# Attention backward for grouped queries: pieces of dV and dK with two heads and four rows c instead of four heads and two

## The chip, the cores and the metric

The kernel runs on one core of one Trainium2 chip. The metric is the time of one execution on the device, in microseconds; the median of several executions is compared.

## The reference

For each of 32 batches there are 32 query heads of 4 rows, 4 key and value heads of 2048 rows, and a head dimension of 128, all bf16. Eight query heads share one key head. The kernel returns the attention's output and the gradients of q, k and v.

```python
B, Hq, Hkv, Sq, Sk, D = 32, 32, 4, 4, 2048, 128
def _fwd_reference(q, k, v):
    k = jnp.repeat(k, rep, axis=1)
    v = jnp.repeat(v, rep, axis=1)
    scores = jnp.einsum("bhqd,bhkd->bhqk", q, k) * D ** -0.5
    p = _softmax(scores, axis=-1)
    return jnp.einsum("bhqk,bhkd->bhqd", p, v)
def reference(q, k, v, grad_out):
    _out, _vjp = jax.vjp(_f, q, k, v)
    _grads = _vjp(grad_out)
    return (_out0, *[jnp.asarray(_g) for _g in _grads])
```

## The kernel before

**Layout.** A batch's 32 heads by 4 rows of q fill the 128 partitions: 32 partitions (G) for each key head h. Key row number p*16 + c of a head is partition p, place c (C = 16). So k and v of a batch are tiles of 128 partitions by 4 heads by 16 c by 128, 2 MB each, loaded by SP in four transfers (LK, LV; L154 and L160).

**Steps.** A batch b goes through named steps, each a small function; a table maps the names to the functions. QDT turns q and grad_out (PE transposes, copied by DVE). KT0 to KT7 and VT0 to VT7 turn k and v in pieces of eight 128x128 blocks (L181, copied by DVE at L183). Sa and Sb are the scores, two halves of 1024 columns (c 0 to 7 and 8 to 15), with a maximum on DVE; EXa and EXb are the exponentials on ACT, into `e0` and `e1`. ETa and ETb turn `e` (L248); O multiplies it with v (L264), writes the output, and forms `delta`. dPa and dPb multiply grad_out with turned v, and DVE makes `ds0` and `ds1` from it (L338). dSTa, dSTb turn `ds` (L248); dQ multiplies it with k. NRM makes the reciprocals and, on POOL, the tiles `dop` and `qp` (L231): grad_out and q scaled by row, each key head's 32 partitions in one of two columns blocks, so that heads 0 and 1 lie in partitions 0 to 63 and heads 2 and 3 in partitions 64 to 127, the rest zero.

**The pieces that are changed.** dV0 to dV7 and dK0 to dK7 call `outer`. dV is `e` transposed times `dop`, dK is `ds` transposed times `qp`. Each piece takes two PSUM banks, runs four matmuls (L303) with 64 partitions of contraction and 256 columns, copies the 128x1024 result on ACT into an output tile (L307), and gives the banks back. In the kernel before, a piece i holds all four heads for c = 2i and 2i + 1: for each c one matmul on partitions 0 to 63 (heads 0, 1; `a = 0`) and one on partitions 64 to 127 (heads 2, 3; `a = 1`), each `a` into its own bank. One output tile holds a batch's dV or dK (16 KB a partition); there are four such tiles (`outp`). When the eighth piece is copied, two stores of 1 MB go out on POOL's queue, one for each pair of heads (L326). In the last batch each half of c is stored when its four pieces are copied (L319).

**Order.** All steps stand in an order written out by hand: HEAD for the first three batches, STEADY once for each batch, TAIL for the last five. Within STEADY, steps of the next batch (`+`), the batch before (`-`) and the one after next (`+2`) are interleaved; each engine runs its part in that order. POOL's queue carries NRM's multiplications, the stores of all outputs, and every fourth batch's loads of q and grad_out.

`Banks` deals out the eight PSUM banks in that order when the program is built; the tile framework puts in the waits between engines.

Of the kernel before, what the change touches and what calls it, by code (L numbers as in the profile page):

```python
# [9 lines left out]
BF16 = mybir.dt.bfloat16  # L10
# [5 lines left out]

HEAD = """
LK@0 LV@0 QDT@0 KT4@0 KT6@0 KT2@0 KT0@0 KT3@0 KT5@0 KT1@0 KT7@0 LK@1 LV@1 VT2@0 Sa@0 Sb@0 VT5@0 VT3@0 EXb@0 VT4@0 EXa@0 VT0@0 QDT@1 KT4@1
KT6@1 KT2@1 KT0@1 NRM@0 ETb@0 ETa@0 VT7@0 KT3@1 VT6@0 VT1@0 dV7@0 O@0 dV5@0 dPb@0 dV1@0 KT5@1 KT1@1 dV3@0 dV6@0 dPa@0 KT7@1 dV2@0 LK@2 LV@2
VT2@1 dV4@0 Sa@1 dV0@0 Sb@1 dK7@0 VT5@1 VT3@1 EXb@1 dSTa@0 VT4@1 EXa@1 VT0@1 QDT@2 dSTb@0 KT4@2 dK1@0 dK6@0 KT6@2 KT2@2 KT0@2 NRM@1 dK0@0 dQ@0  # L20
dK3@0 dK5@0 dK2@0 ETb@1 ETa@1 VT7@1 KT3@2 VT6@1 VT1@1 dV7@1 dK4@0 O@1 dV5@1 dPb@1 dV1@1 KT5@2 KT1@2 dV3@1 dV6@1 dPa@1 KT7@2 dV2@1 LK@3 LV@3
VT2@2 dV4@1 Sa@2 dV0@1 Sb@2 dK7@1 VT5@2 VT3@2 EXb@2 dSTa@1 VT4@2 EXa@2 VT0@2 QDT@3 dSTb@1 KT4@3 dK1@1 dK6@1 KT6@3 KT2@3 KT0@3 NRM@2 dK0@1 dQ@1
dK3@1 dK5@1 dK2@1 ETb@2 ETa@2 VT7@2 KT3@3 VT6@2 VT1@2 dV7@2 dK4@1 O@2 dV5@2 dPb@2 dV1@2 KT5@3 KT1@3 dV3@2 dV6@2 dPa@2 KT7@3 dV2@2 LK@4 LV@4
VT2@3 dV4@2 Sa@3 dV0@2 Sb@3 dK7@2 VT5@3 VT3@3 EXb@3
"""
HEAD_ITERATIONS = 3

STEADY = """
dSTa- VT4 EXa VT0 QDT+ dSTb- KT4+ dK1- dK6- KT6+ KT2+ KT0+ NRM dK0- dQ- dK3- dK5- dK2- ETb ETa VT7 KT3+ VT6 VT1
dV7 dK4- O dV5 dPb dV1 KT5+ KT1+ dV3 dV6 dPa KT7+ dV2 LK+2 LV+2 VT2+ dV4 Sa+ dV0 Sb+ dK7 VT5+ VT3+ EXb+  # L30
"""

TAIL = """
dSTa@-6 VT4@-5 EXa@-5 VT0@-5 QDT@-4 dSTb@-6 KT4@-4 dK1@-6 dK6@-6 KT6@-4 KT2@-4 KT0@-4 NRM@-5 dK0@-6 dQ@-6 dK3@-6 dK5@-6 dK2@-6 ETb@-5 ETa@-5 VT7@-5 KT3@-4 VT6@-5 VT1@-5
dV7@-5 dK4@-6 O@-5 dV5@-5 dPb@-5 dV1@-5 KT5@-4 KT1@-4 dV3@-5 dV6@-5 dPa@-5 KT7@-4 dV2@-5 LK@-3 LV@-3 VT2@-4 dV4@-5 Sa@-4 dV0@-5 Sb@-4 dK7@-5 VT5@-4 VT3@-4 EXb@-4
dSTa@-5 VT4@-4 EXa@-4 VT0@-4 QDT@-3 dSTb@-5 KT4@-3 dK1@-5 dK6@-5 KT6@-3 KT2@-3 KT0@-3 NRM@-4 dK0@-5 dQ@-5 dK3@-5 dK5@-5 dK2@-5 ETb@-4 ETa@-4 VT7@-4 KT3@-3 VT6@-4 VT1@-4
dV7@-4 dK4@-5 O@-4 dV5@-4 dPb@-4 dV1@-4 KT5@-3 KT1@-3 dV3@-4 dV6@-4 dPa@-4 KT7@-3 dV2@-4 LK@-2 LV@-2 VT2@-3 dV4@-4 Sa@-3 dV0@-4 Sb@-3 dK7@-4 VT5@-3 VT3@-3 EXb@-3
dSTa@-4 VT4@-3 EXa@-3 VT0@-3 QDT@-2 dSTb@-4 KT4@-2 dK1@-4 dK6@-4 KT6@-2 KT2@-2 KT0@-2 NRM@-3 dK0@-4 dQ@-4 dK3@-4 dK5@-4 dK2@-4 ETb@-3 ETa@-3 VT7@-3 KT3@-2 VT6@-3 VT1@-3  # L40
dV7@-3 dK4@-4 O@-3 dV5@-3 dPb@-3 dV1@-3 KT5@-2 KT1@-2 dV3@-3 dV6@-3 dPa@-3 KT7@-2 dV2@-3 LK@-1 LV@-1 VT2@-2 dV4@-3 Sa@-2 dV0@-3 Sb@-2 dK7@-3 VT5@-2 VT3@-2 EXb@-2
dSTa@-3 VT4@-2 EXa@-2 VT0@-2 QDT@-1 dSTb@-3 KT4@-1 dK1@-3 dK6@-3 KT6@-1 KT2@-1 KT0@-1 NRM@-2 dK0@-3 dQ@-3 dK3@-3 dK5@-3 dK2@-3 ETb@-2 ETa@-2 VT7@-2 KT3@-1 VT6@-2 VT1@-2
dV7@-2 dK4@-3 O@-2 dV5@-2 dPb@-2 dV1@-2 KT5@-1 KT1@-1 dV3@-2 dV6@-2 dPa@-2 KT7@-1 dV2@-2 VT2@-1 dV4@-2 Sa@-1 dV0@-2 Sb@-1 dK7@-2 VT5@-1 VT3@-1 EXb@-1 dSTa@-2 VT4@-1
EXa@-1 VT0@-1 dSTb@-2 dK1@-2 dK6@-2 NRM@-1 dK0@-2 dQ@-2 dK3@-2 dK5@-2 dK2@-2 ETb@-1 ETa@-1 VT7@-1 VT6@-1 VT1@-1 dV7@-1 dK4@-2 O@-1 dV5@-1 dPb@-1 dV1@-1 dV3@-1 dV6@-1
dPa@-1 dV2@-1 dV4@-1 dV0@-1 dK7@-1 dSTa@-1 dSTb@-1 dK1@-1 dK6@-1 dK0@-1 dQ@-1 dK3@-1 dK5@-1 dK2@-1 dK4@-1
"""
TAIL_ITERATIONS = 5

# [33 lines left out]
def kernel(ctx: ExitStack, tc: tile.TileContext, q, k, v, grad_out, out_0, out_1, out_2, out_3):  # L82
    nc = tc.nc
    B, Hq, Sq, D = q.shape
    NH, Sk = k.shape[1], k.shape[2]
    P = 128
    G = Hq * Sq // NH
    C = Sk // P
# [12 lines left out]
    et_pool = ctx.enter_context(tc.tile_pool(name="etp", bufs=2))  # L101
    ds_pool = ctx.enter_context(tc.tile_pool(name="dsp", bufs=2))
    dst_pool = ctx.enter_context(tc.tile_pool(name="dstp", bufs=2))
    out_pool = ctx.enter_context(tc.tile_pool(name="outp", bufs=4))
    io_pool = ctx.enter_context(tc.tile_pool(name="iop", bufs=3))
    qd_pool = ctx.enter_context(tc.tile_pool(name="qdp", bufs=2))
    sm_pool = ctx.enter_context(tc.tile_pool(name="smp", bufs=3))
# [2 lines left out]
    banks = Banks(ps_pool.tile([P, 8, 512], FP32, name="banks"))  # L110
# [21 lines left out]
    store = nc.gpsimd  # L132
# [158 lines left out]

    def outer(S, x, y, dst, name, i, b, copy):

        if name not in S:
            S[name + "left"] = 8
            S[name] = out_pool.tile([P, NH, C, D], BF16, name=name, tag="outp")
        t = banks.take(2)
        ps = banks.ap(t).rearrange("p a (j c d) -> p a j c d", j=2, c=2)
        for c in range(2):
            u = P * ((2 * i + c) % 8)  # L300
            for a in range(2):
                r = slice(2 * G * a, 2 * G * a + 2 * G)
                nc.tensor.matmul(  # L303
                    ps[:, a, :, c, :], lhsT=S[f"{x}{i // 4}"][r, u:u + P], rhs=S[y][r, :, :],
                    start=True, stop=True, tile_position=(2 * G * a, 0),
                )
        copy(  # L307
            out=S[name][:, :, 2 * i:2 * i + 2, :].rearrange("p h c d -> p h (c d)"),
            in_=banks.ap(t).rearrange("p a (j w) -> p (a j) w", j=2),
        )  # L310
        banks.give(t)
        S[name + "left"] -= 1
        if b == B - 1:

            half = f"{name}half{i // 4}"
            S[half] = S.get(half, 4) - 1
            if S[half] == 0:
                c = slice(8 * (i // 4), 8 * (i // 4) + 8)
                store.dma_start(  # L319
                    out=dst[b].rearrange("p h (c d) -> p h c d", d=D)[:, :, c, :].rearrange("p h c d -> p h (c d)"),  # L320
                    in_=S[name][:, :, c, :].rearrange("p h c d -> p h (c d)"),
                )
        elif S[name + "left"] == 0:
            o = S.pop(name)
            for a in range(2):
                store.dma_start(out=dst[b][:, 2 * a:2 * a + 2, :], in_=o[:, 2 * a:2 * a + 2].rearrange("p h c d -> p h (c d)"))  # L326

    def dV(b, i, copy=nc.scalar.copy):
        outer(st[b], "e", "dop", dv_v, "dv", i, b, copy)

    def dK(b, i, copy=nc.scalar.copy):
        outer(st[b], "ds", "qp", dk_v, "dk", i, b, copy)
# [21 lines left out]
    for w in STEADY.split():  # L354
        ahead = 0
        for mark, n in (("+3", 3), ("+2", 2), ("+", 1), ("-2", -2), ("-", -1)):
            if w.endswith(mark):
                w, ahead = w[:-len(mark)], n
# [3 lines left out]
    with tc.manual_schedule():  # L362

        for w in HEAD.split():
            w, b = w.split("@")
# [5 lines left out]
        for w in TAIL.split():  # L371
            w, b = w.split("@")
# [31 lines left out]
```

## Time and profile before

| | |
|---|---|
| median of 3 runs | 700.63 us (699.89 to 701.72) |
| the profiled execution's own time | 698.71 us |
| its span, first to last instruction | 696.7 us |
| granted TensorE clock | 0.98 |
| PE matmul busy | 626.0 us (90%) |
| DVE, ACT, POOL busy | 584.5, 569.1, 302.7 us |
| L303 matmuls, dV and dK | 1024 and 1024, busy 99.3 and 86.4 us |
| L307 ACT copies, dV and dK | 256 and 256, mean 1028 and 1025 ns |
| moved by DMA | 274.44 MB, mean 394 GB/s |

The profile is one execution. Busy time of an engine is the union of its instructions' times; matmuls overlap in a pipeline, so a group's busy time is less than its count times its mean. "Granted clock" is the share of TensorE's full clock that the throttle let through. An idle time is named after what ended it, so "PE banks L181 <- ACT dv L307" is PE at line 181 waiting for an ACT copy of line 307. The sum of an engine's busy time says little by itself: what counts is which wait ends last in a stretch.

### The profile page before, as it was taken

Reading aid. Unit: us, or ns where it says so; the run is one execution under the profiler, and the core shown is the slowest. Engines: PE = TensorE matmul, PEld = TensorE weight load, DVE = VectorE, ACT = ScalarE, POOL = GpSimd, SP = SyncE. Lnnn points to the kernel's source line nnn. Section 1 sums busy time; section 2 is a strip of 40 time slices with the busy share of each in tenths; the row PEclk is TensorE's granted clock in tenths of the full one; section 3 lists DMA queues with packets and bytes.
Section 4 is the critical chain, followed back from the end, with each engine's and each line's share of the span. In section 5 each row is a group of like instructions: output and inputs, shape, how many; then the busy total and the mean of one; then the engine's idle time right before and its main releaser. Section 6 shows DMA issues by size and latency. Waiting matters only on the chain.

```text
span 696.7 us, 28064 instructions
## 1 busy us (share of the span) xinstructions
PE 626.0 (90%) x12352; PEld 454.1 (65%) x12352; DVE 584.5 (84%) x992; ACT 569.1 (82%) x673; POOL 302.7 (43%) x506
## 2 busy tenths in 40 slices
PE   5899999999998989979999798998998889998982
PEld 4577776677676656666666676667766677666661
DVE  5999999999997998869988688888988869898960
ACT  0698989899887989869888687887888868888994
POOL 1355443555454435443354424544434543345452
PEclk9999999999999999999999899999999989999997
DMA  9989999999999999999999999999999999999767
GB/s 339 400 317 411 417 415 416 416 413 415 417 415 417 414 417 416 417 409 412 415 415 413 373 397 398 400 410 382 416 416 417 415 340 393 415 414 415 289 257 274
DMA packets 75577, 274.44 MB, mean 394 GB/s; under 512 B 8448, under 2 KB 8448, under 8 KB 75456
## 3 DMA queue, kind: packets, MB, share of 16 engines
q0 software_dynamic: 37536, 138.16, 49.3%
q1 hardware_dynamic: 37920, 134.50, 48.9%
q8 instruction: 96, 1.57, 0.8%
q14 instruction: 25, 0.20, 0.1%
HBM read 136.31 MB, written 136.31 MB: 391 GB/s over the span
## 4 chain that ended last, share of the span: by engine, by line
PE 43%; DMA 33%; ACT 6%; DVE 5%; POOL 5%; issue 5%; SPq 0%; POOLq 0%; DVEq 0%; ACTq 0%
PE banks L181 18%; DMA k_sb<-in_k_dram 15%; DMA out_dram<-dk 12%; PE banks L303 10%; PE banks L264 7%; ACT dv L307 5%; PE banks L248 5%; DMA out_dram<-dv 4%; PE banks L198 3%; POOL dop L231 2%; DMA v_sb<-in_v_dram 2%; DVE kt L183 2%; DVE ds L338 1%; ACT dk L307 1%; POOL qp L231 1%
## 5 line engine op out<-in xcount | busy, mean ns | idle before, releaser
L307 ACT CAST dv<-banks 128x1024 bf16<-128x1024 f32 x256 | 245.5, 1028 | 56.9 <-PE banks L303 56.3
L307 ACT CAST dk<-banks 128x1024 bf16<-128x1024 f32 x256 | 250.7, 1025 | 34.5 <-PE banks L303 23.6
L183 DVE COPY kt<-banks 128x1024 bf16<-128x1024 bf16 x256 | 164.3, 680 | 8.3 <-PE banks L181 8.3
L183 DVE COPY vt<-banks 128x1024 bf16<-128x1024 bf16 x256 | 166.2, 680 | 1.3 <-PE banks L181 0.9
L181 PE MATMUL banks<-ident,k_sb 128*128 128x128 bf16 x2048 | 145.8, 221 | 13.1 <-DMA k_sb<-in_k_dram 8.6
L181 PE MATMUL banks<-ident,v_sb 128*128 128x128 bf16 x2048 | 143.5, 220 | 14.3 <-ACT dv L307 9.7
L231 POOL TENSOR_SCALAR dop<-do_sb,rinv 32x128 bf16<-32x128 bf16 x128 | 76.7, 599 | 181.3 <-PE banks L303 118.9
L181 PEld LDWEIGHTS <-k_sb 128*128 128x128 bf16 x2048 | 120.8, 99 | 41.9 <-issue 31.7
L181 PEld LDWEIGHTS <-v_sb 128*128 128x128 bf16 x2048 | 122.2, 98 | 28.7 <-issue 23.3
L303 PE MATMUL banks<-dop,e 64*128 64x256 bf16 x1024 | 99.3, 276 | 15.1 <-POOL dop L231 11.3
L326 POOL DMA_DIRECT2D out_dram<-dv x62 | 43.7, 709 | 138.0 <-ACT dv L307 67.6
L338 DVE SCALAR_TENSOR_TENSOR ds<-banks,delta,e 128x1024 bf16<-128x1024 f32 x64 | 82.2, 1284 | 17.3 <-PE banks L198 14.3
L303 PE MATMUL banks<-qp,ds 64*128 64x256 bf16 x1024 | 86.4, 272 | 2.1 <-ACT dk L307 1.4
L231 POOL TENSOR_SCALAR qp<-q_sb,srinv 32x128 bf16<-32x128 bf16 x128 | 78.1, 610 | 10.7
L222 ACT ACTIVATE e<-banks,negb 128x1024 bf16<-128x1024 f32 x64 | 70.7, 1111 | 8.6 <-DVE negb L214 8.5
L211 DVE TENSOR_REDUCE m<-banks 128x1 f32<-128x1024 f32 x64 | 75.1, 1215 | 0.9 <-PE banks L198 0.9
L303 PEld LDWEIGHTS <-e 64*128 64x128 bf16 x1024 | 34.0, 94 | 63.1 <-issue 46.7
L250 DVE COPY et<-banks 128x1024 bf16<-128x1024 bf16 x64 | 41.3, 686 | 29.6 <-PE banks L248 29.6
L303 PEld LDWEIGHTS <-ds 64*128 64x128 bf16 x1024 | 42.2, 94 | 28.8 <-ACT dv L307 13.1
L326 POOL DMA_DIRECT2D out_dram<-dk x62 | 44.0, 713 | 13.6 <-DMA out_dram<-dk 13.0
L250 DVE COPY dst<-banks 128x1024 bf16<-128x1024 bf16 x64 | 43.5, 681 | 5.5 <-PE banks L248 3.6
L248 PE MATMUL banks<-ident,ds 128*128 128x128 bf16 x512 | 39.4, 221 | 7.1 <-ACT dk L307 6.8
(39 smaller groups left out, 484.1 us busy)
## 6 DMA issues: line engine op xcount, KB each, us to landing
k_sb<-in_k_dram SPq DMA_DIRECT2D x128, 512.0 KB, 13.8
v_sb<-in_v_dram SPq DMA_DIRECT2D x128, 512.0 KB, 18.6
out_dram<-dv POOLq DMA_DIRECT2D x64, 1024.0 KB, 23.6
out_dram<-dk POOLq DMA_DIRECT2D x64, 1024.0 KB, 22.1
out_dram<-o_sb POOLq DMA_DIRECT2D x32, 32.0 KB, 23.2
out_dram<-dq_sb POOLq DMA_DIRECT2D x32, 32.0 KB, 16.2
q_sb<-in_q_dram POOLq DMA_DIRECT2D x7, 128.0 KB, 21.9
do_sb<-in_grad_out_dram POOLq DMA_DIRECT2D x7, 128.0 KB, 22.0
```

The costliest lines, as they stand in the source:

```text
L181: nc.tensor.transpose(out=ps[:, 4 * hh + j, :], in_=S[which][:, 2 * (i % 2) + hh, 4 * (i // 2) + j, :], identity=ident[:])
L183: nc.vector.tensor_copy(out=S[f"{which}t{i}"][:], in_=ps)
L211: nc.vector.reduce_max(out=S["m"][:, i:i + 1], in_=S[f"s{i}"][1], axis=AX.X)
L222: nc.scalar.activation(out=S[f"e{i}"][:], in_=ps, func=ACT.Exp, bias=S["negb"][:], scale=scale, accum_out=S["l"][:, i:i + 1],)
L231: nc.gpsimd.tensor_scalar(out=t[r, h % 2, :], in0=src[r, :], scalar1=by[r, :], scalar2=None, op0=ALU.mult)
L248: nc.tensor.transpose(out=ps[:, u, :], in_=S[f"{src}{i}"][:, P * u:P * u + P], identity=ident[:])
L250: nc.vector.tensor_copy(out=S[f"{name}{i}"][:], in_=ps)
L264: nc.tensor.matmul(ps[G * h:G * h + G, :], lhsT=S[f"{xt}{c // 8}"][:, c % 8, G * h:G * h + G], rhs=S[kv][:, h, c, :], start=(c == 0), stop ...
L303: nc.tensor.matmul(ps[:, a, :, c, :], lhsT=S[f"{x}{i // 4}"][r, u:u + P], rhs=S[y][r, :, :], start=True, stop=True, tile_position=(2 * G * ...
L307: copy(out=S[name][:, :, 2 * i:2 * i + 2, :].rearrange("p h c d -> p h (c d)"), in_=banks.ap(t).rearrange("p a (j w) -> p (a j) w", j=2),)
L326: store.dma_start(out=dst[b][:, 2 * a:2 * a + 2, :], in_=o[:, 2 * a:2 * a + 2].rearrange("p h c d -> p h (c d)"))
L338: nc.vector.scalar_tensor_tensor(out=S[f"ds{i}"][:], in0=ps, scalar=S["delta"][:], in1=S[f"e{i}"][:], op0=ALU.subtract, op1=ALU.mult,)
```

## The change

A piece now holds two heads (`a`, its half of the heads) and four rows c. Pieces 0 to 3 are heads 0 and 1, pieces 4 to 7 heads 2 and 3. All four matmuls of a piece use the same 64 partitions; c 0 and 1 of the piece go to its first bank, 2 and 3 to its second. An output tile holds two heads (8 KB a partition), there are eight of them, and each is stored with one transfer of 1 MB when its four pieces are copied. The last batch is stored in the same way as the others.

In the order, the pieces' slots stay where they were, and their numbers change so that pieces run from 0 to 7: dV7 dV5 dV1 dV3 dV6 dV2 dV4 dV0 becomes dV0 to dV7, and dK7 dK1 dK6 dK0 dK3 dK5 dK2 dK4 becomes dK0 to dK7. HEAD and TAIL are renumbered likewise.

```diff
 STEADY = """
-dSTa- VT4 EXa VT0 QDT+ dSTb- KT4+ dK1- dK6- KT6+ KT2+ KT0+ NRM dK0- dQ- dK3- dK5- dK2- ETb ETa VT7 KT3+ VT6 VT1
-dV7 dK4- O dV5 dPb dV1 KT5+ KT1+ dV3 dV6 dPa KT7+ dV2 LK+2 LV+2 VT2+ dV4 Sa+ dV0 Sb+ dK7 VT5+ VT3+ EXb+
+dSTa- VT4 EXa VT0 QDT+ dSTb- KT4+ dK1- dK2- KT6+ KT2+ KT0+ NRM dK3- dQ- dK4- dK5- dK6- ETb ETa VT7 KT3+ VT6 VT1
+dV0 dK7- O dV1 dPb dV2 KT5+ KT1+ dV3 dV4 dPa KT7+ dV5 LK+2 LV+2 VT2+ dV6 Sa+ dV7 Sb+ dK0 VT5+ VT3+ EXb+
 """
...
-    out_pool = ctx.enter_context(tc.tile_pool(name="outp", bufs=4))
+    out_pool = ctx.enter_context(tc.tile_pool(name="outp", bufs=8))
...
     def outer(S, x, y, dst, name, i, b, copy):
-        if name not in S:
-            S[name + "left"] = 8
-            S[name] = out_pool.tile([P, NH, C, D], BF16, name=name, tag="outp")
+        a, i = i // 4, i % 4
+        half = f"{name}{a}"
+        if half not in S:
+            S[half + "left"] = 4
+            S[half] = out_pool.tile([P, 2, C, D], BF16, name=name, tag="outp")
         t = banks.take(2)
-        ps = banks.ap(t).rearrange("p a (j c d) -> p a j c d", j=2, c=2)
-        for c in range(2):
-            u = P * ((2 * i + c) % 8)
-            for a in range(2):
-                r = slice(2 * G * a, 2 * G * a + 2 * G)
-                nc.tensor.matmul(
-                    ps[:, a, :, c, :], lhsT=S[f"{x}{i // 4}"][r, u:u + P], rhs=S[y][r, :, :],
-                    start=True, stop=True, tile_position=(2 * G * a, 0),
-                )
+        ps = banks.ap(t).rearrange("p x (j c d) -> p x j c d", j=2, c=2)
+        r = slice(2 * G * a, 2 * G * a + 2 * G)
+        for c in range(4):
+            u = P * ((4 * i + c) % 8)
+            nc.tensor.matmul(
+                ps[:, c // 2, :, c % 2, :], lhsT=S[f"{x}{i // 2}"][r, u:u + P], rhs=S[y][r, :, :],
+                start=True, stop=True, tile_position=(2 * G * a, 0),
+            )
         copy(
-            out=S[name][:, :, 2 * i:2 * i + 2, :].rearrange("p h c d -> p h (c d)"),
-            in_=banks.ap(t).rearrange("p a (j w) -> p (a j) w", j=2),
+            out=S[half][:, :, 4 * i:4 * i + 4, :].rearrange("p j (x c) d -> p x j (c d)", x=2),
+            in_=ps.rearrange("p x j c d -> p x j (c d)"),
         )
         banks.give(t)
-        S[name + "left"] -= 1
-        if b == B - 1:
-            half = f"{name}half{i // 4}"
-            S[half] = S.get(half, 4) - 1
-            if S[half] == 0:
-                c = slice(8 * (i // 4), 8 * (i // 4) + 8)
-                store.dma_start(
...
-                )
-        elif S[name + "left"] == 0:
-            o = S.pop(name)
-            for a in range(2):
-                store.dma_start(out=dst[b][:, 2 * a:2 * a + 2, :], in_=o[:, 2 * a:2 * a + 2].rearrange("p h c d -> p h (c d)"))
+        S[half + "left"] -= 1
+        if S[half + "left"] == 0:
+            o = S.pop(half)
+            store.dma_start(out=dst[b][:, 2 * a:2 * a + 2, :], in_=o[:].rearrange("p h c d -> p h (c d)"))
```

More of the change, by code (lines that the diff above doesn't have):

```diff
@@ L18 @@
 LK@0 LV@0 QDT@0 KT4@0 KT6@0 KT2@0 KT0@0 KT3@0 KT5@0 KT1@0 KT7@0 LK@1 LV@1 VT2@0 Sa@0 Sb@0 VT5@0 VT3@0 EXb@0 VT4@0 EXa@0 VT0@0 QDT@1 KT4@1
[L19 to L24, printed above, removed]
+KT6@1 KT2@1 KT0@1 NRM@0 ETb@0 ETa@0 VT7@0 KT3@1 VT6@0 VT1@0 dV0@0 O@0 dV1@0 dPb@0 dV2@0 KT5@1 KT1@1 dV3@0 dV4@0 dPa@0 KT7@1 dV5@0 LK@2 LV@2
+VT2@1 dV6@0 Sa@1 dV7@0 Sb@1 dK0@0 VT5@1 VT3@1 EXb@1 dSTa@0 VT4@1 EXa@1 VT0@1 QDT@2 dSTb@0 KT4@2 dK1@0 dK2@0 KT6@2 KT2@2 KT0@2 NRM@1 dK3@0 dQ@0
+dK4@0 dK5@0 dK6@0 ETb@1 ETa@1 VT7@1 KT3@2 VT6@1 VT1@1 dV0@1 dK7@0 O@1 dV1@1 dPb@1 dV2@1 KT5@2 KT1@2 dV3@1 dV4@1 dPa@1 KT7@2 dV5@1 LK@3 LV@3
+VT2@2 dV6@1 Sa@2 dV7@1 Sb@2 dK0@1 VT5@2 VT3@2 EXb@2 dSTa@1 VT4@2 EXa@2 VT0@2 QDT@3 dSTb@1 KT4@3 dK1@1 dK2@1 KT6@3 KT2@3 KT0@3 NRM@2 dK3@1 dQ@1
+dK4@1 dK5@1 dK6@1 ETb@2 ETa@2 VT7@2 KT3@3 VT6@2 VT1@2 dV0@2 dK7@1 O@2 dV1@2 dPb@2 dV2@2 KT5@3 KT1@3 dV3@2 dV4@2 dPa@2 KT7@3 dV5@2 LK@4 LV@4
+VT2@3 dV6@2 Sa@3 dV7@2 Sb@3 dK0@2 VT5@3 VT3@3 EXb@3
 """
@@ L28 @@
 STEADY = """
-dSTa- VT4 EXa VT0 QDT+ dSTb- KT4+ dK1- dK6- KT6+ KT2+ KT0+ NRM dK0- dQ- dK3- dK5- dK2- ETb ETa VT7 KT3+ VT6 VT1
-dV7 dK4- O dV5 dPb dV1 KT5+ KT1+ dV3 dV6 dPa KT7+ dV2 LK+2 LV+2 VT2+ dV4 Sa+ dV0 Sb+ dK7 VT5+ VT3+ EXb+
+dSTa- VT4 EXa VT0 QDT+ dSTb- KT4+ dK1- dK2- KT6+ KT2+ KT0+ NRM dK3- dQ- dK4- dK5- dK6- ETb ETa VT7 KT3+ VT6 VT1
+dV0 dK7- O dV1 dPb dV2 KT5+ KT1+ dV3 dV4 dPa KT7+ dV5 LK+2 LV+2 VT2+ dV6 Sa+ dV7 Sb+ dK0 VT5+ VT3+ EXb+
 """
 TAIL = """
-dSTa@-6 VT4@-5 EXa@-5 VT0@-5 QDT@-4 dSTb@-6 KT4@-4 dK1@-6 dK6@-6 KT6@-4 KT2@-4 KT0@-4 NRM@-5 dK0@-6 dQ@-6 dK3@-6 dK5@-6 dK2@-6 ETb@-5 ETa@-5 VT7@-5 KT3@-4 VT6@-5 VT1@-5
@@ L37 @@
[L37 to L44, printed above, removed]
@@ L45 @@
-dPa@-1 dV2@-1 dV4@-1 dV0@-1 dK7@-1 dSTa@-1 dSTb@-1 dK1@-1 dK6@-1 dK0@-1 dQ@-1 dK3@-1 dK5@-1 dK2@-1 dK4@-1
+dSTa@-6 VT4@-5 EXa@-5 VT0@-5 QDT@-4 dSTb@-6 KT4@-4 dK1@-6 dK2@-6 KT6@-4 KT2@-4 KT0@-4 NRM@-5 dK3@-6 dQ@-6 dK4@-6 dK5@-6 dK6@-6 ETb@-5 ETa@-5 VT7@-5 KT3@-4 VT6@-5 VT1@-5
+dV0@-5 dK7@-6 O@-5 dV1@-5 dPb@-5 dV2@-5 KT5@-4 KT1@-4 dV3@-5 dV4@-5 dPa@-5 KT7@-4 dV5@-5 LK@-3 LV@-3 VT2@-4 dV6@-5 Sa@-4 dV7@-5 Sb@-4 dK0@-5 VT5@-4 VT3@-4 EXb@-4
+dSTa@-5 VT4@-4 EXa@-4 VT0@-4 QDT@-3 dSTb@-5 KT4@-3 dK1@-5 dK2@-5 KT6@-3 KT2@-3 KT0@-3 NRM@-4 dK3@-5 dQ@-5 dK4@-5 dK5@-5 dK6@-5 ETb@-4 ETa@-4 VT7@-4 KT3@-3 VT6@-4 VT1@-4
@@ new lines @@
+dV0@-4 dK7@-5 O@-4 dV1@-4 dPb@-4 dV2@-4 KT5@-3 KT1@-3 dV3@-4 dV4@-4 dPa@-4 KT7@-3 dV5@-4 LK@-2 LV@-2 VT2@-3 dV6@-4 Sa@-3 dV7@-4 Sb@-3 dK0@-4 VT5@-3 VT3@-3 EXb@-3
+dSTa@-4 VT4@-3 EXa@-3 VT0@-3 QDT@-2 dSTb@-4 KT4@-2 dK1@-4 dK2@-4 KT6@-2 KT2@-2 KT0@-2 NRM@-3 dK3@-4 dQ@-4 dK4@-4 dK5@-4 dK6@-4 ETb@-3 ETa@-3 VT7@-3 KT3@-2 VT6@-3 VT1@-3
+dV0@-3 dK7@-4 O@-3 dV1@-3 dPb@-3 dV2@-3 KT5@-2 KT1@-2 dV3@-3 dV4@-3 dPa@-3 KT7@-2 dV5@-3 LK@-1 LV@-1 VT2@-2 dV6@-3 Sa@-2 dV7@-3 Sb@-2 dK0@-3 VT5@-2 VT3@-2 EXb@-2
+dSTa@-3 VT4@-2 EXa@-2 VT0@-2 QDT@-1 dSTb@-3 KT4@-1 dK1@-3 dK2@-3 KT6@-1 KT2@-1 KT0@-1 NRM@-2 dK3@-3 dQ@-3 dK4@-3 dK5@-3 dK6@-3 ETb@-2 ETa@-2 VT7@-2 KT3@-1 VT6@-2 VT1@-2
@@ L46 @@
+dV0@-2 dK7@-3 O@-2 dV1@-2 dPb@-2 dV2@-2 KT5@-1 KT1@-1 dV3@-2 dV4@-2 dPa@-2 KT7@-1 dV5@-2 VT2@-1 dV6@-2 Sa@-1 dV7@-2 Sb@-1 dK0@-2 VT5@-1 VT3@-1 EXb@-1
+dSTa@-2 VT4@-1 EXa@-1 VT0@-1 dSTb@-2 dK1@-2 dK2@-2 NRM@-1 dK3@-2 dQ@-2 dK4@-2 dK5@-2 dK6@-2 ETb@-1 ETa@-1 VT7@-1 VT6@-1 VT1@-1 dV0@-1 dK7@-2 O@-1 dV1@-1 dPb@-1 dV2@-1
+dV3@-1 dV4@-1 dPa@-1 dV5@-1 dV6@-1 dV7@-1 dK0@-1
+dSTa@-1 dSTb@-1 dK1@-1 dK2@-1 dK3@-1 dQ@-1 dK4@-1 dK5@-1 dK6@-1 dK7@-1
 """
@@ L307, in outer @@
         copy(
-            out=S[name][:, :, 2 * i:2 * i + 2, :].rearrange("p h c d -> p h (c d)"),
-            in_=banks.ap(t).rearrange("p a (j w) -> p (a j) w", j=2),
+            out=S[half][:, :, 4 * i:4 * i + 4, :].rearrange("p j (x c) d -> p x j (c d)", x=2),
+            in_=ps.rearrange("p x j c d -> p x j (c d)"),
         )
         banks.give(t)
-        S[name + "left"] -= 1
-        if b == B - 1:
-            half = f"{name}half{i // 4}"
-            S[half] = S.get(half, 4) - 1
-            if S[half] == 0:
-                c = slice(8 * (i // 4), 8 * (i // 4) + 8)
-                store.dma_start(
-                    out=dst[b].rearrange("p h (c d) -> p h c d", d=D)[:, :, c, :].rearrange("p h c d -> p h (c d)"),
-                    in_=S[name][:, :, c, :].rearrange("p h c d -> p h (c d)"),
-                )
-        elif S[name + "left"] == 0:
-            o = S.pop(name)
-            for a in range(2):
-                store.dma_start(out=dst[b][:, 2 * a:2 * a + 2, :], in_=o[:, 2 * a:2 * a + 2].rearrange("p h c d -> p h (c d)"))
+        S[half + "left"] -= 1
```

## The prediction

> **What bounds the kernel now.** I read the page first (shares of the engines, the slices over time), then busy times in two windows, then PE in the timeline, then PE's waits in one window.
>
> ```profile
> PE 626.0 (90%) x12352; PEld 454.1 (65%) x12352; DVE 584.5 (84%) x992; ACT 569.1 (82%) x673; POOL 302.7 (43%) x506
> ...
> GB/s 339 400 317 411 417 415 416 416 413 415 417 415 417 414 417 416 417 409 412 415 415 413 373 397 398 400 410 382 416 416 417 415 340 393 415 414 415 289 257 274
> ```
>
> The GB/s row never passes 417. The kernel moves 274.44 MB, 8.576 MB for each of 32 batches, so at 416 GB/s a batch cannot be faster than 20.6 us. PE is the busiest engine, and where it is busy changes over the run:
>
> ```profile
> 36.00:213.00 177.00, 172.25 (x3474) 125.49 (x3472) 163.48 (x280) 159.41 (x190) 84.57 (x139) 1.00 1.02 407
> 213.00:645.00 432.00, 393.18 (x7729) 284.33 (x7727) 366.62 (x622) 356.40 (x423) 188.36 (x310) 0.98 1.02 406
> ```
>
> The columns are the stretch, its length, then busy time of PE, PEld, DVE, ACT, POOL, granted clock, DMA share and GB/s. The timeline has one QDT transpose a batch; they start at 36.23, 213.46 and 645.07 us. The first stretch is nine batches of 19.69 us, faster than the transfers allow: four output buffers and loaded inputs let the stores fall behind. PE is busy 97% there, at clock 1.00. The second stretch is twenty batches of 21.58 us; the stores' debt has come due, transfers set the pace and PE is idle 9%. So PE's own pace is 19.7 us a batch, the transfers' is 20.6, and PE has about 1 us a batch to give away before it sets the whole run.
>
> **What a piece costs on PE.** These are PE rows of the timeline (start, length, group, count):
>
> ```profile
> 56.18 0.61 PE L181 MATMUL banks<-ident,k_sb 128*128 128x128 bf16 x8
> ...
> 57.42 1.50 PE L181 MATMUL banks<-ident,k_sb 128*128 128x128 bf16 x24
> 58.85 0.39 PE L303 MATMUL banks<-qp,ds 64*128 64x256 bf16 x4
> ...
> 60.19 0.83 PE L303 MATMUL banks<-qp,ds 64*128 64x256 bf16 x12
> ...
> 67.64 0.61 PE L303 MATMUL banks<-dop,e 64*128 64x256 bf16 x8
> ```
>
> Transposes of 128 columns: 16 more cost 1.50 - 0.61 = 0.89 us, 0.056 us each, so 256 columns stream in 0.11 us. Four matmuls of 256 columns in a row should then add 0.45 us. At L303 eight more add 0.83 - 0.39 = 0.44 us: four add 0.22. They therefore run two at a time, the `a = 0` one on rows 0 to 63 and the `a = 1` one on rows 64 to 127. A row of the first batch, where the pair was split, agrees:
>
> ```profile
> 23.84 0.27 PE L303 MATMUL banks<-dop,e 64*128 64x256 bf16 x1 [0.21 <-POOL dop L231]
> 25.20 0.38 PE L303 MATMUL banks<-dop,e 64*128 64x256 bf16 x3 [1.10 <-POOL dop L231]
> ```
>
> One alone lasts 0.27 (0.16 of it the pipeline's end), three last 0.38: one single round and one shared by two would do that, three rounds in series would need 0.49.
>
> **Part 1, two heads and four rows c.** The piece still has four matmuls of 256 columns, two banks and one ACT copy of 128x1024. But all four now use the same row half `r`, so no two of them can share the array. A piece goes from two rounds to four: +0.22 us, 16 pieces a batch, +3.52 us. Where pieces of opposite halves stand next to each other the last round of one can run beside the first of the other; the order has two such places a batch (dV0 dK7-, and dV3 dV4), -0.22. Net +3.30 us a batch. No load of weights should show: L303's two matmuls of the same half already follow each other at 0.11 us with theirs hidden.
>
> Is it covered? PE's idle time at its own pace is 177 - 172.25 = 4.75 us in nine batches, 0.53 each. Its waits there:
>
> ```profile
> PE banks L181 <- ACT dv L307: 3.0, 9, 0.4
> PE banks L181 <- issue: 0.5, 1, 0.5
> ```
>
> The first, 0.33 us a batch, is VT5 wanting a bank that ACT still copies out of. With PE slower by 0.22 a piece and ACT not, it goes. So PE's pace becomes 19.69 + 3.30 - 0.33 = 22.66 us; if all idle time goes, 22.46. That is above 20.6, so transfers no longer set the pace, and the waits of the second stretch (POOL's dop 10.0 us in all, L248 on ACT 6.8, k_sb 5.4) should mostly fade: they come with full queues. I take 22.5. From 36.2 to 645.1 lie 29 batches: 29 x 22.5 = 652.5 in place of 608.9, **+43.6 us**.
>
> Ahead of 36.2 lie nine pieces: +2.0, less the 1.1 us wait shown above, because dV0 now reads only rows 0 to 63 of dop and starts after two of POOL's four multiplications: **+0.9**. From 645 to 671 one batch of pieces: **+3.3**. From 671 to 688 ACT is busy 16.14 of 17.00 us and PE 9.93, so PE's sixteen slower pieces hide behind copies: **0** (up to +1.5 if ACT starves between pieces).
>
> **Part 2, eight tiles of 8 KB.** Same 1 MB stores, same 62+2 for each output, same bytes of buffer. The store of a first half leaves after its fourth piece, about half a batch earlier; a buffer is reused after two batches as before. In POOL's queue dk's first store now stands between NRM and dQ's store and waits for the copy of dK3-, with only dQ's and dk's next store behind it; dv's first store stands ahead of every fourth batch's q_sb and do_sb loads, which are needed over a batch later. Both cost nothing while three io buffers and that batch cover them; if not, a dop some 1.2 us late now and then, as in the 11.3 us that PE waits for it today. The copy writes four runs of 256 columns at other addresses; I take the row's 1028 ns unchanged (no row shows another stride; a 5% slower copy is 18.7 us of ACT a batch, still under PE).
>
> **Part 3, the last batch.** Today it stores halves of c in short runs, and both halves of dk finish together: the last two stores go out at 687.01 and 687.93 and land at 696.7. With the change only dk's second MB is left. One MB at 416 GB/s is 2.5 us, against 8.8: between -6 and 0; I take **-3**.
>
> **Part 4, the order.** Pieces keep their slots, so banks are taken in the same order. dK0 now needs the first half of ds (from dPa) where dK7 needed the second (from dPb): at 316 us ds of dPa is written by 318.17 and the slot starts at 319.97, so 1.8 us to spare. Both halves of e are ready before dV0. **0**.
>
> Sum: 43.6 + 0.9 + 3.3 - 3 = +44.8 us on 698.7 (span 696.7 and 2.0 around it), 743.5. The median of the runs is 1.9 above that execution; half of it is added, since a kernel bound by PE should scatter less: **745 us**.
>
> **Rivals.**
> *Transfers still bound (faster or equal).* If the extra rounds fit in PE's idle time, what is left is better placed stores. The price if so: slices at 340, 373, 382 fill up, perhaps half of the 37 us between 696.7 and 274.44 MB at 416 GB/s (660): from 682 to 700, say 690. For it: the 393 of 432. Against: it decides at a PE pace of 20.6, and even with all idle time gone PE needs 22.46. Chance 0.04.
> *Copies bound.* ACT's copies, 16 x 1.03 = 16.4 us of 17.8 busy a batch (569.1/32), would set the pace, and the pairs would have bought nothing: about 701 us. Against: ACT idles 10% in the first stretch, where PE idles 3%. Chance 0.03. The Trainium skill, "TensorEngine Tiling (Array Packing)", PSUM Bottleneck, warns of this: packing speeds up TensorE but not the emptying of PSUM, which may become the bottleneck. By that rule the pairs are free to lose; the trace agrees only in the last 17 us.
> *PE's extra plus new waits.* Four rounds of one half, then a copy: ACT gets its bank 0.22 later each time, and in runs such as dV6 Sa dV7 Sb dK0 VT5 the bank comes back later still. If each of 16 pieces passes on another 0.05 to 0.1 us, the pace is 23.5 to 24: 770 to 785. Against: today the copy is the slower side in these runs, and it gets slack. Chance 0.11.
> The forecast itself: 0.82.
>
> One more risk is the clock: in 350 to 400 and 550 to 600 us the granted clock is 0.96 and 0.93, together with PE's waits. I expect 1.00 throughout, as in the first stretch, where PE hardly waits; 0.98 all along would cost 2% of PE's time, some 14 us, within the range. The Trainium skill, "TensorE: Matmul & The Clock Gate", HAM oscillation, says that PE gaps over about 3.4 us drop the clock, so by that page nothing is lost here; the trace does not bear out the length, since its longest PE wait in those stretches is 2.4 us.
>
> **Numbers.** The forecast's own range is 22.0 to 23.0 us a batch (728 to 759); with the first part of the third rival, 728 to 765. A measurement can tell about 0.3%, 2 us, from no change: faster 0.04, same 0.02, slower 0.94.
>
> **What would show it.** Right: L303 groups of four at 0.6 us in place of 0.39; L303's PE busy near twice 99.3 + 86.4; PE over 95% busy in every slice; GB/s near 380; POOL's waits for stores gone; batches of 22.5 us from the first to the last. Wrong: four still in 0.39 us, or batches near 20.6 at 416 GB/s, or PE idle on ACT in each batch.

## The result and the profile after

The changed kernel takes 715.67 us (median of 4 runs, 715.05 to 716.71) against 700.26 us: a ratio of 1.0218, 95% interval 1.0202 to 1.0234. It is slower, as forecast, but by 15 us where 45 were forecast, and 715.67 lies below the range of 728 to 765. The profiled execution took 715.05 us, its span is 713.2.

From the page of the changed kernel:

```profile
PE 690.0 (97%) x12352; PEld 515.7 (72%) x12352; DVE 585.1 (82%) x992; ACT 578.1 (81%) x673; POOL 302.5 (42%) x506
...
GB/s 340 409 314 396 406 397 387 399 405 404 401 387 402 406 399 406 405 387 399 386 382 410 389 404 385 403 395 402 405 396 394 379 412 416 400 381 398 296 218 293
```

PE is busy 97% of the span, 64 us more than before; DVE and POOL are where they were, and ACT is busy 9 us more. The transfers now run mostly at 380 to 410 GB/s, where before they stood at 415 to 417. The same two stretches as before, cut at whole batches (length, then PE, PEld, DVE, ACT, POOL busy, clock, DMA share, GB/s):

```profile
36.00:209.00 173.00, 172.32 (x3110) 128.96 (x3107) 147.24 (x251) 145.28 (x170) 75.39 (x124) 1.00 1.00 389
209.00:661.00 452.00, 449.36 (x8090) 335.03 (x8088) 382.57 (x650) 378.25 (x440) 197.53 (x325) 1.00 1.02 398
```

There is no second regime any more. QDT's transposes start at 36.03 and 661.07 us, 29 batches of 21.55 us on average, and nearly all of them are 21.5. The granted clock is 1.00 in both stretches.

The pieces themselves, in PE's timeline:

```profile
295.05 1.04 PE L306 MATMUL banks<-qp,ds 64*128 64x256 bf16 x8
...
297.47 0.61 PE L306 MATMUL banks<-qp,ds 64*128 64x256 bf16 x4
...
303.22 0.28 PE L306 MATMUL banks<-dop,e 64*128 64x256 bf16 x1
303.23 0.28 PE L306 MATMUL banks<-qp,ds 64*128 64x256 bf16 x1
303.34 0.27 PE L306 MATMUL banks<-dop,e 64*128 64x256 bf16 x1
303.35 0.27 PE L306 MATMUL banks<-qp,ds 64*128 64x256 bf16 x1
303.45 0.27 PE L306 MATMUL banks<-dop,e 64*128 64x256 bf16 x1
303.46 0.27 PE L306 MATMUL banks<-qp,ds 64*128 64x256 bf16 x1
303.56 0.27 PE L306 MATMUL banks<-dop,e 64*128 64x256 bf16 x1
303.57 0.27 PE L306 MATMUL banks<-qp,ds 64*128 64x256 bf16 x1
...
307.40 0.62 PE L306 MATMUL banks<-dop,e 64*128 64x256 bf16 x8
```

Four matmuls of one half last 0.61 us where a piece lasted 0.39: two rounds became four, as the prediction had it, and two pieces of the same half in a row (dK1 dK2 at 295.05) last 1.04, eight rounds. But dV0 and dK7, which stand behind each other in PE's program as four matmuls of `dop,e` and then four of `qp,ds`, start in turns, about 0.01 us apart, and are through in four rounds together. dV3 and dV4 at 307.40 do the same: eight matmuls in 0.62. The prediction gave such a place one shared round; it shares all four. (A round is one matmul's 0.11 us on its half of the rows, with or without a partner on the other half.)

### The profile page after: what moved, and what is told of

It reads as the page before. It is cut to its first block, busy times and chain, and to the rows that moved or that the text cites. A ratio compares the mean times of both kernels' runs of the same rounds, so it can differ in the third digit from the quotient of the medians.

```text
span 713.2 us, 28147 instructions
## 1 busy us (share of the span) xinstructions
PE 690.0 (97%) x12352; PEld 515.7 (72%) x12352; DVE 585.1 (82%) x992; ACT 578.1 (81%) x673; POOL 302.5 (42%) x506
## 4 chain that ended last, share of the span: by engine, by line
PE 81%; DMA 6%; ACT 5%; issue 2%; DVE 2%; POOL 2%; SPq 0%; POOLq 0%; ACTq 0%; DVEq 0%
PE banks L306 28%; PE banks L182 28%; PE banks L249 9%; PE banks L199 8%; PE banks L265 8%; DMA out_dram<-dk 6%; ACT dk L310 4%; DVE kt L184 1%; DMA k_sb<-in_k_dram 1%; DVE m L212 1%; ACT dv L310 1%; POOL dop L232 1%; PE banks L172 0%; POOL qp L232 0%; POOL out_dram L318 0%
## 5 line engine op out<-in xcount | busy, mean ns | idle before, releaser
L310 ACT CAST dv<-banks 128x1024 bf16<-128x1024 f32 x256 | 249.1, 1023 | 62.4 <-PE banks L306 59.6
L310 ACT CAST dk<-banks 128x1024 bf16<-128x1024 f32 x256 | 249.9, 1022 | 45.8 <-DVE qdt L174 21.5
L182 PE MATMUL banks<-ident,k_sb 128*128 128x128 bf16 x2048 | 143.6, 222 | 3.4 <-DMA k_sb<-in_k_dram 1.9
L182 PE MATMUL banks<-ident,v_sb 128*128 128x128 bf16 x2048 | 140.6, 219 | 0.7 <-DMA v_sb<-in_v_dram 0.2
L306 PE MATMUL banks<-qp,ds 64*128 64x256 bf16 x1024 | 139.3, 271 | 0.8 <-ACT dk L310 0.5
L306 PE MATMUL banks<-dop,e 64*128 64x256 bf16 x1024 | 136.6, 271 | 0.7 <-ACT dv L310 0.3
L182 PEld LDWEIGHTS <-v_sb 128*128 128x128 bf16 x2048 | 120.6, 98 | 13.7 <-issue 8.9
L306 PEld LDWEIGHTS <-ds 64*128 64x128 bf16 x1024 | 84.2, 94 | 34.1 <-issue 14.7
L318 POOL DMA_DIRECT2D out_dram<-dv x64 | 45.3, 708 | 147.7 <-ACT dv L310 147.7
L306 PEld LDWEIGHTS <-e 64*128 64x128 bf16 x1024 | 70.2, 94 | 49.9 <-issue 28.1
L330 DVE SCALAR_TENSOR_TENSOR ds<-banks,delta,e 128x1024 bf16<-128x1024 f32 x64 | 82.2, 1284 | 21.3 <-PE banks L199 21.2
L318 POOL DMA_DIRECT2D out_dram<-dk x64 | 46.8, 732 | 8.8 <-ACT dq_sb L289 3.0
## 6 DMA issues: line engine op xcount, KB each, us to landing
out_dram<-dv POOLq DMA_DIRECT2D x64, 1024.0 KB, 12.6
```

The source lines that it names most:

```text
L182: nc.tensor.transpose(out=ps[:, 4 * hh + j, :], in_=S[which][:, 2 * (i % 2) + hh, 4 * (i // 2) + j, :], identity=ident[:])
L306: nc.tensor.matmul(ps[:, c // 2, :, c % 2, :], lhsT=S[f"{x}{i // 2}"][r, u:u + P], rhs=S[y][r, :, :], start=True, stop=True, tile_position ...
L310: copy(out=S[half][:, :, 4 * i:4 * i + 4, :].rearrange("p j (x c) d -> p x j (c d)", x=2), in_=ps.rearrange("p x j c d -> p x j (c d)"),)
L318: store.dma_start(out=dst[b][:, 2 * a:2 * a + 2, :], in_=o[:].rearrange("p h c d -> p h (c d)"))
L330: nc.vector.scalar_tensor_tensor(out=S[f"ds{i}"][:], in0=ps, scalar=S["delta"][:], in1=S[f"e{i}"][:], op0=ALU.subtract, op1=ALU.mult,)
```

## The experiments

### Neighbours taken apart, and more of them made

Both keep the changed kernel and only renumber the pieces in their slots.

```diff
     for n, f in (("KT", KT), ("VT", VT), ("dV", dV), ("dK", dK)):
-        table[f"{n}{i}"] = lambda b, f=f, i=i: f(b, i)
+        p = {"dV": [0, 1, 4, 2, 3, 5, 6, 7], "dK": [4, 5, 6, 7, 0, 1, 2, 3]}.get(n, range(8))[i]
+        table[f"{n}{i}"] = lambda b, f=f, i=p: f(b, i)
```

> The changed kernel with its pieces renumbered so that no two pieces of opposite halves stand next to each other on PE (dV's slots hold pieces 0 1 4 2 3 5 6 7, dK's hold 4 5 6 7 0 1 2 3). Theory (two neighbouring pieces of opposite halves run side by side, all four rounds): the two places a batch that shared are lost, 8 rounds of 0.109 us, batches of 21.5 + 0.87 = 22.4 us, in all about 716 + 30 x 0.87 = 742 us. Rival (only the last round of one and the first of the other share, as the prediction had it, and the rest of the miss are waits that went away): 2 rounds, 21.7 us a batch, about 722 us.

Measured: 740.18 us, ratio 1.0557 (1.0540 to 1.0574), batches of 22.34 us. In its timeline the slots that shared now stand in series:

```profile
296.09 1.04 PE L306 MATMUL banks<-dop,e 64*128 64x256 bf16 x8
...
313.78 0.61 PE L306 MATMUL banks<-dop,e 64*128 64x256 bf16 x4
314.23 0.60 PE L306 MATMUL banks<-qp,ds 64*128 64x256 bf16 x4
```

The group at 296.09 is the fourth and fifth slot of dV, now two pieces of the lower half: 1.04 us where the changed kernel had 0.62. The dK piece at 314.23 starts 0.45 us after the dV piece before it, where it started 0.01 us after. Taking the two places apart costs 0.79 us a batch (22.34 - 21.55): 8 rounds of 0.109 are 0.87, and one round each would have been 0.22. The rival is out.

> The changed kernel with dK's slots holding pieces 0 1 4 2 5 3 6 7, so that two more places a batch have pieces of opposite halves as neighbours (the second with the third slot, the fifth with the sixth). Theory: 8 rounds fewer, PE's pace 21.5 - 0.87 = 20.65 us a batch, as slow as the transfers' 20.6; 690 to 702 us. Rival (one round at each place): 21.3 us a batch, about 709 us.

Here dK's list is 0 1 4 2 5 3 6 7 and dV's is unchanged. Measured: 703.78 us, ratio 1.0031 (1.0011 to 1.0052). The typical batch is 20.64 us, 0.86 less than the changed kernel's 21.50: eight rounds again, as the theory has it. The total is 2 us above its range; in the profiled execution (705.28 us, the longest of its ten) four batches of 23.3 to 24.2 us stand late in the run. PE's waits name a part of the reason:

```profile
PE banks L172 <- DMA q_sb<-in_q_dram: 8.2, 4, 3.0
PE banks L172 <- DMA do_sb<-in_grad_out_dram: 2.8, 5, 0.7
```

(us in total, times, longest; 3.1 us of the first row also stand at the start of the run in the changed kernel.) The loads of q and grad_out stand in POOL's queue behind a store of dv; POOL waited 14.1 us for stores of dv ahead of the do_sb loads, and PE got them too late.

### The old piece with its loops exchanged

```diff
-        for c in range(2):
-            u = P * ((2 * i + c) % 8)
-            for a in range(2):
+        for a in range(2):
+            for c in range(2):
+                u = P * ((2 * i + c) % 8)
```

> The kernel before with the loops over c and a exchanged: a piece's four matmuls come as lower half, lower half, upper half, upper half. Theory (a matmul of the free half does not wait for earlier matmuls of the other half): still two rounds, four in 0.39 us, 700 us. Rival (matmuls start in program order): three rounds, four in 0.50 us, PE's own pace 19.7 + 1.75 = 21.4 us a batch, about 712 us.

Measured: 699.54 us, ratio 0.9986 (0.9967 to 1.0006): no difference. Its pieces:

```profile
59.24 0.40 PE L303 MATMUL banks<-qp,ds 64*128 64x256 bf16 x4
...
60.58 0.83 PE L303 MATMUL banks<-qp,ds 64*128 64x256 bf16 x12
```

Two rounds a piece, the same as when the halves alternate in the program. So the third matmul of a piece, in the free half, does not wait for the second.

This run also speaks against a rival that the starts above leave open, that the matmuls of two pieces had been put in turns when the program was built. In 26 batches the four matmuls of dV7 start ahead of those of dK4, which stands behind it; in the five batches in which the second half of dV7 waits for `dop`, the order is another:

```profile
225.17 0.39 PE L303 MATMUL banks<-dop,e 64*128 64x256 bf16 x2
225.87 0.27 PE L303 MATMUL banks<-dop,e 64*128 64x256 bf16 x1 [0.31 <-POOL dop L231]
225.88 0.28 PE L303 MATMUL banks<-qp,ds 64*128 64x256 bf16 x1
225.98 0.27 PE L303 MATMUL banks<-dop,e 64*128 64x256 bf16 x1
226.00 0.46 PE L303 MATMUL banks<-qp,ds 64*128 64x256 bf16 x3
```

While dV7's third matmul waits for `dop`, none behind it starts; then dK4's first, on the half that dV7 has left, starts 0.01 us after it and ahead of dV7's fourth.

### The old output tiles under the new pieces

```diff
-    out_pool = ctx.enter_context(tc.tile_pool(name="outp", bufs=8))
+    out_pool = ctx.enter_context(tc.tile_pool(name="outp", bufs=4))
...
-        S[half + "left"] -= 1
-        if S[half + "left"] == 0:
-            o = S.pop(half)
-            store.dma_start(out=dst[b][:, 2 * a:2 * a + 2, :], in_=o[:].rearrange("p h c d -> p h (c d)"))
+        S[name + "left"] -= 1
+        if S[name + "left"] == 0:
+            o = S.pop(name)
+            for a in range(2):
+                store.dma_start(out=dst[b][:, 2 * a:2 * a + 2, :], in_=o[:, 2 * a:2 * a + 2].rearrange("p h c d -> p h (c d)"))
```

> The changed pieces and order with the old output tiles: four tiles of 16 KB, both stores of an output after its eighth piece. Theory (PE sets the pace, the place of the stores is free): batches of 21.5 us, 716 us, within 2 us; the end no more than 2.5 us later, since two stores of 1 MB are left at the end. Rival (the earlier stores of half tiles gave part of the time back by keeping the queues short): POOL's waits for stores return and the time is 720 us or more.

Measured: 716.31 us, ratio 1.0221 (1.0196 to 1.0246), beside 1.0218 of the changed kernel, and no wait of POOL for a store comes back. The tiles and the earlier stores are worth nothing that can be measured while PE sets the pace; the 15 us come from the pieces and from the order of their numbers.

### PE's own pace in the kernel before

```diff
         elif S[name + "left"] == 0:
             o = S.pop(name)
             for a in range(2):
-                store.dma_start(...)
+                if name == "dk" or b < 2: store.dma_start(...)
```

> The kernel before with dV's stores left out for batches 2 to 30 (dV of these batches is computed and not written out). It takes away a quarter of the transfers and some of POOL's issues and leaves PE's work as it was. Theory (PE's own pace is 19.5 to 19.7 us a batch, and in the kernel before the full queues cost the 21.0 that it has on average): batches of 19.5 to 19.7 us throughout, about 655 us. Rival (PE's pace slackens later in the run for another reason, such as its clock): batches of over 20.5 us after 213 us as before, 685 us or more.

Measured in one execution: 662.95 us. Batches from 36.5 us on are 19.75 us on average (19.4 to 21.2), where the kernel before has 21.0, so the theory holds in the main; the total is 8 us above it, in part because some batches are 20 to 21 us. PE's pace with a quarter of the transfers, and POOL's issues of these stores, out of its way is thus 19.4 us in the quickest batches and 19.75 on average, and the full queues cost the kernel before about 1.25 us a batch. That is the slack that hid part of the change.

### The loads of q and grad_out

These look for a version that beats both kernels. The first pair of runs issues the loads of every fourth batch from SP:

```diff
-            GROUP(b // W + 1, nc.gpsimd)
+            GROUP(b // W + 1, nc.sync)
```

> The renumbered kernel with four neighbouring pairs a batch (703.8 us), and the q_sb and do_sb loads of every fourth batch issued from SP in place of POOL. In it PE waited for these loads, and batches of 23.3 to 24.2 us came every fourth batch at the end. Theory (these loads stand behind stores in POOL's full queue): the late batches fall to 20.6 us, 690 to 697 us. Rival (the full transfers themselves cost it, wherever the loads are issued): 701 to 705 us.

> The kernel before with the same loads issued from SP. Theory: its slow batches (24.6 and 25.9 us, where POOL stood 4 us at each issue and dop came late) get shorter, 690 to 697 us; rival: 699 to 702 us.

Measured: 719.82 us (1.0286, 1.0249 to 1.0322) and 710.85 us (1.0152, 1.0124 to 1.0180). Both theories fall, and not to their rivals: both are slower. PE's waits of the second kernel:

```profile
PE banks L181 <- DMA k_sb<-in_k_dram: 33.2, 11, 9.1
```

In the kernel before, this row is 8.6 us with 2.1 at most. The wait for dop did fall, from 11.3 to 1.3 us, as the theory had it; this one took its place. On SP the small loads share a queue with those of k and v; single batches of 29 to 36 us stand in the two kernels, and the one in which PE stood 9 us for k_sb is among them. What in SP's queue holds k back was not followed further.

> The changed pieces and tiles with all sixteen pieces of a batch in eight neighbouring pairs of opposite halves (slots moved next to each other, dQ ahead of dK3, numbers 0 1 4 2 5 3 6 7), and the q and grad_out loads from SP. Theory: 32 rounds of 0.109 us a batch as in the kernel before and fewer switches between matmul shapes, PE's pace 18.5 to 19.5 us, the transfers' 20.6 us set the time: 685 to 697 us. Rival (pairs take four banks at once, and ACT empties them one after the other, so PE waits for banks): batches of 21 us or more, 705 us or more.

Measured: 707.51 us (1.0114, 1.0079 to 1.0148), typical batches 21.1 us: the rival, by both its numbers. These rows, from the profiled execution (714.39 us, the longest of its six), show its mechanism, two of PE's waits first and then PE and ACT in one batch:

```profile
PE banks L181 <- ACT dv L309: 17.9, 25, 0.7
PE banks L248 <- ACT dk L309: 13.8, 31, 0.6
...
112.05 1.02 ACT L309 CAST dk<-banks 128x1024 bf16<-128x1024 f32 x1
112.56 1.17 PE L305 MATMUL banks<-dop,e 64*128 64x256 bf16 x8
114.66 0.62 PE L305 MATMUL banks<-dop,e 64*128 64x256 bf16 x8
```

About 32 us of waits for banks that ACT still empties, where the changed kernel has under 2. And pairs come apart: the one at 114.66 lasts 0.62 us, the one at 112.56 lasts 1.17, because its second piece starts only at 113.12, 0.05 us after the end of ACT's copy. Such a delay inside a pair is in no row of waits, since PE is busy with the first piece. The total is not the price of the pairs alone: the loads are on SP here too, and one batch of this profile is 26.9 us long.

The last pair leaves the loads on POOL and issues them two batches earlier:

```diff
-        if b % W == W - 1 and b + 1 < B:
+        if b % W == 1 and b + W < B:
```

> The renumbered kernel with four neighbouring pairs a batch (703.8 us), with the q_sb and do_sb loads still on POOL but issued two batches earlier. In it PE waited at QDT for these loads, and four late batches were 23.3 to 24.2 us long. Theory (PE waits for these loads alone): the four fall to 20.6 to 21.5 us, 691 to 700 us, about level with or faster than the kernel before. Rival (POOL's issues in a full queue hold back other things as well): 701 to 705 us.

> The kernel before with the same loads issued two batches earlier. There PE did not wait for these loads but for dop, which is late since POOL stands some 4 us at each issue. Theory: the issues still stand, 698 to 702 us. Rival (the loads themselves): 694 us or less.

Measured: 699.02 us for the first, ratio 0.9979 (0.9965 to 0.9993), and 700.35 us for the second, 0.9993 (0.9981 to 1.0005). In the first PE no longer waits for q_sb after the start:

```profile
PE banks L182 <- DMA k_sb<-in_k_dram: 3.4, 3, 1.4
PE banks L306 <- POOL dop L232: 3.2, 3, 2.3
PE banks L172 <- DMA q_sb<-in_q_dram: 3.1, 1, 3.1
```

Against 703.78 us for the same order with late loads, some 4 to 5 us came back (the two were timed in different sets of runs). It is the fastest version of the changed pieces, 1.6 us below the kernel before: 0.2%, too little to be called faster, though its interval lies below 1. The second stays as it was, as its theory had it; its slowest batches are still 23.6 to 25.8 us long.

## Why the prediction was wrong in size, point by point

**What bounds the kernel.** Right: PE became the bound, and the full queues that had made 21.6 us a batch no longer did. The dv store's median time to landing fell from 23.6 to 12.6 us, and POOL's waits behind stores (35.1 + 22.1 + 17.4 us before, in the rows named after out_dram<-dk and out_dram<-dv) are gone.

**A piece costs two rounds more.** Right: 0.61 us for four matmuls. Sixteen such pieces in series, with no shared place, were measured as the kernel with its neighbours apart: 740.18 us. The sign that L303's busy time would come near twice 99.3 + 86.4 us did not come: it is 136.6 + 139.3, 1.5 times. The shared rounds count once, and the 0.16 us at the end of each group did not double.

**Two shared places a batch, -0.22 us.** This step failed. It let the halves overlap only where the last matmul of one piece meets the first of the next, which is what starts in the order of the program would give. They do not start in that order: each place shares four rounds, and the two together -0.87 us. The difference of three rounds of 0.109 at two places is 0.65 us a batch, 19 of the 29 us of the miss; by the 0.79 us that taking the neighbours apart cost it would be 0.57, or 17. The prediction's pair at 67.64 could not show this, since there the halves alternate in the program.

The Trainium skill, "TensorE: Matmul & The Clock Gate", Step-by-step: what each phase is for, has only weight loads pulled ahead and matmuls in program order; the rows at 303.22 to 303.57 show otherwise for matmuls in opposite halves, and the measurement decides. The Trainium skill, "TensorEngine Tiling (Array Packing)", Key Properties, has tiles load weights and multiply independently of each other; with that the trace agrees.

**Waits that go.** Sized too small. 22.5 us a batch was forecast; with the shared rounds put right it would be 21.85, and 21.55 was measured: 0.3 us, 9 us over 29 batches. PE's idle time fell from 0.53 to about 0.08 us a batch (0.68 us in eight batches), close to the 0.49 that 22.5 had taken off. The rest was time in which groups were stretched without PE counting as idle: O's group in the batch at 55.6 us was 1.24 us long before, and is 1.08 now:

```profile
64.27 1.24 PE L264 MATMUL banks<-v_sb,et 128*32 128x128 bf16 x64
...
303.77 1.08 PE L265 MATMUL banks<-v_sb,et 128*32 128x128 bf16 x64
```

Over eight batches of the first stretch, the mean time from the start of O's group to the next start was 1.16 us before and is 1.01 now, half of the 0.3; the other half is not traced to a place. The kernel with its neighbours apart has such slack too: 19.69 + 3.49 would be 23.18, and it runs at 22.34.

**The tiles, the queue of POOL, the order: 0.** Right for the tiles and the queue, by the run with the old tiles. The order was priced for banks and for the halves of `ds`, not for which halves become neighbours; other choices brought the time some 12 us down (703.78) or 24 us up (740.18). One part of it held only while the queue was not full: the q and grad_out loads behind dv's first store, costed at nothing, were waited for once PE was back at 20.6 us a batch.

**The last batch, -3 us.** The end lies 8.8 us after the last store's issue before (687.93 to 696.7) and 6.7 us after it now (706.52 to 713.2): -2.1. The choice of -3 came near; the last MB took longer than the 2.5 us of its best case. Over the whole end, from the last QDT on, 51.6 us became 52.1: +0.5 where +3.3 and -3 were forecast. The start, up to the transpose at 36.2, was forecast at +0.9 and came out at -0.2.

**The rivals.** Transfers still bound: out, the typical batch is 21.5 us. Copies bound: out, PE is 97% busy and ACT 81%. New waits at each piece: out, PE's waits fell. None of them was the case that came, a smaller loss of the same kind. **The clock:** 1.00 as expected in both stretches.

## What to carry to other kernels

When row halves of the array are worked in parallel, cost a change by rounds of each half over the whole neighbourhood in PE's queue, not within one group: a piece of one half costs no extra rounds if a piece of the other half stands next to it and has its banks in time. A bound that appears after a change must be compared with the slack of the bound that it replaces, over the whole run: here the queues had been costing about 1.25 us a batch, and that was paid back. A load that is harmless behind a store in an idle queue needs another look once the queue is full.

## What the runs showed of the hardware that was not expected

Matmuls on opposite halves of the rows start out of program order: the first matmul of dK7 starts 0.01 us after the first of dV0, with three matmuls of dV0 still to come, and two such pieces take four rounds, 0.11 us each. With the loops exchanged in the old piece it is the same, 0.40 us for four; in the five batches there in which a matmul of dV7 waited for its data, none behind it started meanwhile. How far ahead in the queue a partner may stand was not measured beyond the four matmuls of a piece. And the queue that a small load stands in can matter: 14 loads of 128 KB moved from POOL to SP cost the kernel before 10 us, and why stays open.
